# Retention and two feed-forward layers: where the decay is applied and which quarters of the array the states use

## The chip, the cores and the metric

The kernel runs on one core of one Trainium2 chip. The metric is the device time of one execution in microseconds. A page of the profile and a trace of one execution stand beside the times. Engines: PE is TensorE's matmul row, PEld its weight loads, DVE is VectorE, ACT is ScalarE, POOL is GpSimd, SP is SyncE, which here only issues DMAs.

## The reference

Four sequences of 768 tokens, 8 heads of 64, float32. Per head a state is carried through the tokens; then two feed-forward layers of 512 to 2048 to 512 follow on the 3072 tokens.

```python
for t in range(S):
    state = gamma[None, :, None, None] * state + np.einsum('bhd,bhe->bhde', k[:, :, t], v[:, :, t])
    y[:, :, t] = scale * np.einsum('bhd,bhde->bhe', q[:, :, t], state)
...
h = x @ w_in;  g = np.maximum(0.01 * h, h);            x = g @ w_out
h = x @ w_in;  g = h * (1.0 / (1.0 + np.exp(-1.702 * h)));  x = g @ w_out
```

## The kernel before, in words

**Retention.** The tokens go in 24 steps of 128 (4 sequences of 6 chunks, `s` is the step, `c` its chunk within the sequence). The 8 heads are 4 pairs `n` of two halves `e`; a pair's two heads of 64 fill the 128 partitions. A step has four groups of matmuls in float32, each of which the trace shows as 16 instructions, two for each of 8 products:

- `a_scores` (L252): keys by queries, 64 rows by 128 columns of the array, into the PSUM tiles `s0` and `s1`. VectorE multiplies each by the decay mask (`sm`, L256).
- `kv` (L283): decayed keys by values, accumulated through a sequence; VectorE multiplies it by a decay to the next state `st` (L298). GpSimd decays the keys beforehand (L267).
- `o` by `sm` (L289): values by masked scores, 128 rows by 64 columns of the array.
- `o` by state (L295): state by queries, 64 by 64 of the array, added into the same `o`. It is there where `c > 0`, in 20 of the 24 steps. Head half `e = 0` lies on rows and columns 0 to 63, `e = 1` on 64 to 127, so two of the array's four quarters are used. The queries were multiplied by their decay before (`qs`, L263, VectorE, two steps ahead).

`a_store` copies `o` out of PSUM with ScalarE. The tile `o` has two buffers. The first four steps' tokens go straight into the split tile `x0` (a high part by ScalarE, L307, and the rest by VectorE, L308); later steps go to DRAM by pairs (L314, L316). From step 4 on one feed-forward group, `ffn_in(0, m)` (L204, 12 matmuls of 512 columns), follows in each step but 8, 13, 18 and 23.

**Weights.** The feed-forward weights come as 64-bit floats and are converted to a pair of float32r parts, one block of 128 by 512 at a time. `work()` (L183) is one conversion: it issues the load for two conversions later (`load_raw`), then `convert` (ScalarE L139, L140; VectorE L141, L142, L144, L146), then `finish` of the conversion before (ScalarE's high part L125, GpSimd's low part L126), then `round_in` (an integer addition on GpSimd, L152). It is called in retention steps 2 to 4 and then in the steps that follow a feed-forward group, 17 times; and 15 times more after the retention, once for each `ffn_out` group of the first block (L486). There two `ffn_out` groups go with one `ffn_in` group until the queue of 10 blocks between them is worked off, near 212 us.

**Order.** Nothing reorders the program: each engine takes its instructions in the order of the source, and waits come from the tiles' buffers. A step `s` of the loop calls: scores of step `s + 1`, `a_out(s)`, `work()` where it is due, `a_store(s)`, the decays for step `s + 2`, the load for step `s + 4`, and the feed-forward group. The memory of the `a_` pools is taken over by the second weight home when the retention is done.

**Start.** The loads stand in SP's queue in this order: queries and keys of step 0, the mask (512 KB), the rest of step 0, the small decays, step 1, the query decay (256 KB), steps 2 and 3, two raw weight blocks. Matmuls on an idle tile fill the gaps.

Of the kernel before, what the change touches and what calls it, by code (L numbers as in the profile page):

```python
# [9 lines left out]
F32 = mybir.dt.float32  # L10
# [73 lines left out]
def retention_two_ffn(ctx: ExitStack, tc: tile.TileContext, qkv, consts, small, w1i, w1o, w2i, w2o, scratch, out):  # L84
# [42 lines left out]

    def load_raw(kind, m, src):
        t = cv_p.tile([P, 512, 2], U32, tag="raw", name="raw", bufs=3)
        nc.sync.dma_start(out=t, in_=src[m].bitcast(U32).rearrange("p (f two) -> p f two", two=2))  # L130
        raw[kind, m] = t
# [51 lines left out]
    def work():  # L183
# [35 lines left out]
    with ExitStack() as actx:  # L219
# [10 lines left out]
        mask = cst[:, :H].rearrange("p (n e) i -> p n e i", e=2)  # L230
# [4 lines left out]
        ins, sc_t, ks_t, qs_t = {}, {}, {}, {}  # L235
# [8 lines left out]
        def a_scores(s):  # L244
# [3 lines left out]
            ps = [ps_a.tile([P, NP, P], F32, tag=f"s{e}", name=f"s{e}") for e in range(2)]  # L248
            for n in range(NP):
                for e in range(2):  # L250
                    r = slice(D * e, D * e + D)
                    nc.tensor.matmul(out=ps[e][:, n], lhsT=kT[r, n], rhs=qT[r, n], start=True, stop=True,  # L252
                                     skip_group_check=True)
# [17 lines left out]
        def a_out(s):  # L271
            b, c = steps[s]
            t = ins.pop(s)
            sm, ks, qs = sc_t.pop(s), ks_t.pop(s, None), qs_t.pop(s, None)
# [10 lines left out]
            o = ps_a.tile([P, NP, P], F32, tag="o", name="o", bufs=2)  # L285
            for n in range(NP):
                for e in range(2):
                    r = slice(D * e, D * e + D)
                    nc.tensor.matmul(out=o[r, n], lhsT=v[:, n, r], rhs=sm[:, e, n], start=(n == 0),  # L289
                                     stop=(c == 0), skip_group_check=True)  # L290
# [11 lines left out]
        def a_store(s, o):  # L302
            blk, cc = divmod(s, CPB)
            cols = slice(cc * P, cc * P + P)
            if blk == 0:

                nc.scalar.copy(out=x0[:, :, 0, cols], in_=o)  # L307
                nc.vector.tensor_tensor(out=x0[:, :, 1, cols], in0=o, in1=x0[:, :, 0, cols].bitcast(F32),  # L308
                                        op=ALU.subtract)
                return  # L310
            if cc % 2 == 0:
                a_store.x = a_x.tile([P, NP, 2 * P], F32, tag="x", name="x")
            x = a_store.x
            nc.scalar.copy(out=x[:, :, cc % 2 * P : cc % 2 * P + P], in_=o)  # L314
            if cc % 2:
                nc.sync.dma_start(out=xd0[blk][:, :, cc * P - P : cc * P + P], in_=x)  # L316
# [16 lines left out]
        warm = ps_a.tile([P, 512], F32, tag="o", name="warm", bufs=2)  # L333
# [10 lines left out]
        for s in range(len(steps)):  # L344
# [574 lines left out]
```

## Time and profile before

| | |
|---|---|
| time, median of 3 runs | 1128.59 us (1128.12 to 1129.69) |
| span of the profiled execution | 1127.0 us |
| TensorE busy | 1103.3 us (98%) |
| VectorE busy | 696.4 us (62%) |
| ScalarE busy | 491.5 us (44%) |
| GpSimd busy | 269.8 us (24%) |
| mean DMA rate | 177 GB/s |

The span runs from the first to the last instruction of one profiled execution; the runs are timed as a whole. A matmul's end in the trace is modelled and matmuls overlap, so a busy TensorE is one that has instructions in flight. In a row of a timeline `x16` counts merged instructions, and the bracket at its end tells how long the engine was idle before it and what ended that.

### The profile page before, as it was taken

Reading aid. Unit: us, or ns where it says so; the run is one execution under the profiler, and the core shown is the slowest. Engines: PE = TensorE matmul, PEld = TensorE weight load, DVE = VectorE, ACT = ScalarE, POOL = GpSimd, SP = SyncE. Lnnn points to the kernel's source line nnn. Section 1 sums busy time; section 2 is a strip of 40 time slices with the busy share of each in tenths; the row PEclk is TensorE's granted clock in tenths of the full one; section 3 lists DMA queues with packets and bytes.
Section 4 is the critical chain, followed back from the end, with each engine's and each line's share of the span. In section 5 each row is a group of like instructions: output and inputs, shape, how many; then the busy total and the mean of one; then the engine's idle time right before and its main releaser. Section 6 shows DMA issues by size and latency. Waiting matters only on the chain.

```text
span 1127.0 us, 16412 instructions
## 1 busy us (share of the span) xinstructions
PE 1103.3 (98%) x6188; PEld 940.3 (83%) x6189; DVE 696.4 (62%) x1034; ACT 491.5 (44%) x823; POOL 269.8 (24%) x269
## 2 busy tenths in 40 slices
PE   8999989999999999999999999999999899999997
PEld 6888867788888888888888899999998688888886
DVE  5977769635555556455441557575654696686784
ACT  2544455444444444445442435343432444545543
POOL 2655446523324233232321111111100000000000
PEclk9999989999999999999999999999999999999999
DMA  9898543225454445354359633436289725326322
GB/s 366 313 339 292 181 148 113 75 89 164 130 179 154 153 157 175 122 172 137 121 174 426 232 113 114 168 113 243 99 282 359 261 76 176 123 76 205 106 64 74
DMA packets 88095, 199.03 MB, mean 177 GB/s; under 512 B 7888, under 2 KB 51920, under 8 KB 82640
## 3 DMA queue, kind: packets, MB, share of 16 engines
q1 hardware_dynamic: 69584, 172.81, 43.9%
q10 hardware_dynamic: 18432, 25.17, 6.2%
q8 instruction: 48, 0.79, 0.3%
q14 instruction: 31, 0.25, 0.1%
HBM read 125.60 MB, written 72.35 MB: 176 GB/s over the span
## 4 chain that ended last, share of the span: by engine, by line
PE 91%; DVE 4%; DMA 2%; issue 1%; ACT 1%; POOL 0%; SPq 0%; ACTq 0%; DVEq 0%; POOLq 0%
PE h L204 22%; PE y L486 22%; PE b L576 9%; PE a L576 6%; PE d L759 6%; PE f L759 6%; PE c L576 6%; PE e L759 5%; PE h L759 3%; PE s L252 2%; PE o L289 2%; PE o L295 2%; PE kv L283 1%; DMA home<-wdo 1%; DVE raw L141 1%
## 5 line engine op out<-in xcount | busy, mean ns | idle before, releaser
L486 PE MATMUL y<-g,home 128*128 128x512 f32 x1008 | 246.2, 395 | 6.5 <-ACT home L125 3.8
L204 PE MATMUL h<-xs,home 128*128 128x512 f32 x1008 | 246.5, 394 | 0.0
L486 PEld LDWEIGHTS y<-g,home 128*128 128x128 f32 x1008 | 190.4, 189 | 50.8 <-POOL home L126 5.1
L204 PEld LDWEIGHTS h<-xs,home 128*128 128x128 f32 x1008 | 188.5, 188 | 43.2 <-issue 2.4
L126 DVE TENSOR_TENSOR g<-h,g 128x512 fp32r<-128x512 f32 x96 | 101.4, 1057 | 156.4 <-ACT g L125 156.2
L710 ACT CAST op<-g 128x512 fp32r<-128x512 f32 x168 | 100.9, 621 | 90.1 <-DVE g L737 42.4
L715 DVE TENSOR_TENSOR op<-g,op 128x512 fp32r<-128x512 f32 x168 | 112.1, 686 | 40.4 <-ACT op L710 39.7
L209 ACT ACTIVATE h<-h 128x512 f32<-128x512 f32 x96 | 57.3, 597 | 170.3 <-PE h L204 168.2
L576 PE MATMUL b<-xf,home 128*128 128x384 f32 x576 | 115.4, 334 | 2.0 <-DVE g L606 1.4
L576 PEld LDWEIGHTS b<-xf,home 128*128 128x128 f32 x576 | 101.1, 188 | 2.7 <-DVE g L606 1.7
L404 POOL TENSOR_TENSOR f<-f,raw 128x512 int32<-128x512 int32 x32 | 41.7, 1303 | 247.6 <-DVE f L400 247.6
L125 ACT CAST g<-h 128x512 fp32r<-128x512 f32 x96 | 59.6, 621 | 78.6 <-PE y L486 78.1
L576 PE MATMUL a<-xf,home 128*128 128x384 f32 x384 | 76.9, 334 | 0.0
L576 PE MATMUL c<-xf,home 128*128 128x384 f32 x384 | 76.9, 334 | 0.0
L759 PE MATMUL d<-op,home 128*128 128x512 f32 x288 | 69.0, 398 | 5.7 <-DVE op L715 5.7
L737 DVE TENSOR_TENSOR g<-g 128x512 f32<-128x512 f32 x96 | 72.3, 753 | 1.9 <-DMA g<-gd 1.9
L410 POOL TENSOR_TENSOR f<-f 128x128 f32<-128x128 f32 x128 | 72.0, 581 | 5.0
L759 PEld LDWEIGHTS d<-op,home 128*128 128x128 f32 x288 | 54.8, 191 | 18.0 <-DVE op L715 6.1
L759 PE MATMUL e<-op,home 128*128 128x512 f32 x288 | 69.3, 395 | 0.1
L576 PEld LDWEIGHTS a<-xf,home 128*128 128x128 f32 x384 | 67.5, 188 | 0.1
L576 PEld LDWEIGHTS c<-xf,home 128*128 128x128 f32 x384 | 67.5, 188 | 0.0
L759 PE MATMUL f<-op,home 128*128 128x512 f32 x288 | 66.9, 391 | 0.0
(94 smaller groups left out, 1400.3 us busy)
## 6 DMA issues: line engine op xcount, KB each, us to landing
gd<-g ACTq DMA_DIRECT2D x128, 192.0 KB, 2.0
g<-gd SPq DMA_DIRECT2D x96, 256.0 KB, 4.6
in<-qkv SPq DMA_DIRECT2D x21, 1024.0 KB, 6.9
home<-wdi SPq DMA_DIRECT2D x8, 1792.0 KB, 13.0
home<-wdo SPq DMA_DIRECT2D x8, 1792.0 KB, 9.8
raw<-w1i SPq DMA_DIRECT2D x16, 512.0 KB, 5.6
raw<-w1o SPq DMA_DIRECT2D x16, 512.0 KB, 3.3
raw<-w2i SPq DMA_DIRECT2D x32, 256.0 KB, 3.6
```

What stands on the lines that cost most here:

```text
L125: nc.scalar.copy(out=hi, in_=src)
L126: (eng or nc.vector).tensor_tensor(out=lo, in0=src, in1=hi.bitcast(F32), op=ALU.subtract)
L204: nc.tensor.matmul(out=h, lhsT=w[:, a, k], rhs=xs[k][:, c], start=(i == 0), stop=(i == 3 * NP - 1))
L209: nc.scalar.activation(out=t, in_=h, func=AF.Lrelu)
L404: nc.gpsimd.tensor_tensor(out=self.f.bitcast(I32), in0=self.f.bitcast(I32), in1=self.low.bitcast(I32), op=ALU.add)
L410: nc.gpsimd.tensor_tensor(out=f[:, o], in0=f[:, a], in1=f[:, b], op=ALU.subtract)
L486: nc.tensor.matmul(out=y[j], lhsT=w[:, a, j * P : j * P + P], rhs=g[:, c], start=(m == 0 and i == 0), stop=(m == KF - 1 and i == 2))
L576: nc.tensor.matmul(out=t, lhsT=w[:, k, a], rhs=x[:, b, k], start=(start and m == 0), stop=(m == 5), skip_group_check=True)
L710: nc.scalar.copy(out=t[:, 0], in_=block_of(raw, *item))
L715: nc.vector.tensor_tensor(out=t[:, 1], in0=block_of(raw, *item), in1=t[:, 0].bitcast(F32), op=ALU.subtract)
L737: nc.vector.tensor_tensor(out=a(*s[0]), in0=a(*s[1]), in1=a(*s[2]), op=s[3])
L759: nc.tensor.matmul(out=t[:, j], lhsT=w[:, j, a], rhs=x[:, b], start=(new and q == 0 and m == 0), stop=(q == NQ - 1 and m == 2), skip_group ...
```

## The change

- The query decay is no longer applied to the queries. Both parts of `o` are made without it, and `a_store` multiplies by it on VectorE while it copies `o` out of PSUM, for every step. In the first four steps ScalarE's high part and VectorE's rest are then taken from that copy.
- The mask then holds only a key's own decay, which is a column of the small table; GpSimd makes the mask on chip from it with one `affine_select`, and the mask's load goes. The small table is issued first, on ScalarE's queue.
- In `o`, odd pairs are put on the swapped halves of the partitions, so that the state products of two neighbouring pairs use the four quarters of the array; even and odd pairs go to different PSUM banks. `o` takes two banks and has one buffer. The rows of the first layer's input weights, and the query decay, are loaded with halves swapped for odd pairs, by three DMAs (`swapped`).
- The two score tiles are one, with one `sm` operation of 1024 elements.
- `round_in` runs on VectorE.
- Where a step has a conversion, `a_store` is called inside `work`, after `convert` and before `finish` and `round_in`.

```diff
+    def swapped(d, s):
+        nc.sync.dma_start(out=d[:, 0::2], in_=s[:, 0::2])
+        for e in range(2):
+            nc.sync.dma_start(out=d[D * e : D * e + D, 1::2], in_=s[D * (1 - e) : D * (1 - e) + D, 1::2])
...
-        nc.gpsimd.tensor_tensor(out=a.bitcast(I32), in0=a.bitcast(I32), in1=t[:, :, 0].bitcast(I32), op=ALU.add)
+        nc.vector.tensor_tensor(out=a.bitcast(I32), in0=a.bitcast(I32), in1=t[:, :, 0].bitcast(I32), op=ALU.add)
...
         if n < len(order):
             convert(*order[n])
+        between()
         if 0 < n <= len(order):
             kind, m = order[n - 1]
             finish(kind, m)
...
-            ps = [ps_a.tile([P, NP, P], F32, tag=f"s{e}", name=f"s{e}") for e in range(2)]
+            ps = ps_a.tile([P, 2, NP, P], F32, tag="s", name="s")
...
-            for e in range(2):
-                nc.vector.tensor_tensor(out=sm[:, e], in0=ps[e], in1=mask[:, :, e], op=ALU.mult)
+            nc.vector.tensor_tensor(out=sm, in0=ps, in1=mask, op=ALU.mult)
...
-            if c > 0:
-                qs_t[s] = a_t.tile([P, NP, P], F32, tag="qs", name="qs")
-                nc.vector.tensor_tensor(out=qs_t[s], in0=ins[s][:, 0].rearrange("p (n i) -> p n i", n=NP),
-                                        in1=qdec, op=ALU.mult)
...
-            o = ps_a.tile([P, NP, P], F32, tag="o", name="o", bufs=2)
+            o = ps_a.tile([P, 2, 512], F32, tag="o", name="o")
+            out = lambda n, e: o[D * (e ^ (n & 1)) : D * (e ^ (n & 1)) + D, n % 2, n // 2 * P : n // 2 * P + P]
...
-                        nc.tensor.matmul(out=o[r, n], lhsT=st[c % 2][r, n], rhs=qs[r, n], start=False, stop=True,
+                        nc.tensor.matmul(out=out(n, e), lhsT=st[c % 2][r, n], rhs=q[r, n], start=False, stop=True,
...
+            if cc % 2 == 0:
+                a_store.x = a_x.tile([P, NP, 2 * P], F32, tag="x", name="x")
+            x = a_store.x[:, :, cc % 2 * P : cc % 2 * P + P]
+            nc.vector.tensor_tensor(out=x.rearrange("p (m u) i -> p u m i", u=2),
+                                    in0=o[:, :, : 2 * P].rearrange("p u (m i) -> p u m i", i=P),
+                                    in1=qdec.rearrange("p (m u) i -> p u m i", u=2), op=ALU.mult)
             if blk == 0:
-                nc.scalar.copy(out=x0[:, :, 0, cols], in_=o)
-                nc.vector.tensor_tensor(out=x0[:, :, 1, cols], in0=o, in1=x0[:, :, 0, cols].bitcast(F32),
+                nc.scalar.copy(out=x0[:, :, 0, cols], in_=x)
+                nc.vector.tensor_tensor(out=x0[:, :, 1, cols], in0=x, in1=x0[:, :, 0, cols].bitcast(F32),
                                         op=ALU.subtract)
                 return
-            nc.scalar.copy(out=x[:, :, cc % 2 * P : cc % 2 * P + P], in_=o)
...
+        nc.scalar.dma_start(out=smalls, in_=small)
         nc.sync.dma_start(out=ins[0][:, :2], in_=qkv[0, :, :2])
-        nc.sync.dma_start(out=cst[:, :H], in_=consts[:, :H])
         nc.sync.dma_start(out=ins[0][:, 2:], in_=qkv[0, :, 2:])
-        nc.sync.dma_start(out=smalls, in_=small)
+        nc.gpsimd.affine_select(out=cst[:, :H], in_=kdec[:, 0].unsqueeze(2).to_broadcast([P, H, P]),
+                                pattern=[[0, H], [1, P]], base=0, channel_multiplier=-1,
+                                compare_op=ALU.is_ge, fill=0.0)
         a_load(1)
-        nc.sync.dma_start(out=cst[:, H:], in_=consts[:, H:])
+        swapped(qdec, consts[:, H:])
...
             if s >= W0 - 2 and done[0] < KF + 1 and (s <= W0 or now_in[s - 1]):
-                work()
-            a_store(s, o)
+                work(lambda: a_store(s, o))
+            else:
+                a_store(s, o)
```

## Rows read from the trace of the kernel before

**Rows 1.** The page: the chain that ended last, shares of the span by engine.
```profile
PE 91%; DVE 4%; DMA 2%; issue 1%; ACT 1%; POOL 0%; SPq 0%; ACTq 0%; DVEq 0%; POOLq 0%
```

**Rows 2.** Windows: length, busy us of PE, PEld, DVE, ACT, POOL; clock, DMA.
```profile
0.00:30.00 30.00, 26.77 (x335) 19.18 (x338) 18.03 (x31) 7.86 (x12) 8.59 (x12) 1.00 0.95 369
30.00:58.00 28.00, 28.00 (x335) 22.69 (x330) 26.33 (x41) 14.06 (x23) 19.14 (x15) 1.00 0.86 311
58.00:141.00 83.00, 83.00 (x964) 67.27 (x963) 60.43 (x96) 35.16 (x62) 42.38 (x32) 1.00 0.75 268
141.00:212.00 71.00, 64.52 (x263) 50.62 (x262) 60.64 (x73) 39.68 (x68) 42.73 (x29) 0.95 0.35 118
...
300.00:350.00 50.00, 50.00 (x220) 41.11 (x219) 29.68 (x41) 24.15 (x39) 14.96 (x21) 1.00 0.49 160
```

**Rows 3.** Timeline, retention step 8: start us, us, engine, line, operation.
```profile
54.17 0.41 DVE L298 TENSOR_TENSOR st<-kv,smalls 128x256 f32<-128x256 f32 x1
...
54.35 0.85 PEld L295 LDWEIGHTS o<-qs,st 64*64 64x64 f32 x16 [0.17 <-issue]
...
54.50 1.31 DVE L141 TENSOR_SCALAR raw<-raw 128x512 uint32<-128x512 uint32 x1
...
56.64 0.69 DVE L146 SCALAR_TENSOR_TENSOR a<-a,raw 128x512 uint32<-128x512 uint32 x1
...
56.98 1.04 PE L289 MATMUL o<-sm,in 128*64 128x128 f32 x16
```

**Rows 4.** Windows of line L295 alone at its start: busy PE, PEld; clock, DMA.
```profile
17.32:17.34 0.02, 0.01 (x2) 0.01 (x2) 1.00 0.50 205
17.35:17.48 0.13, 0.13 (x2) 0.13 (x4) 1.00 1.08 441
```

**Rows 5.** Groups by line, 0 to 212 us: count, busy us, mean ns, idle before.
```profile
L152 POOL TENSOR_TENSOR a<-a,raw 128x512 int32<-128x512 int32 x31 | 48.9, 1576 | 43.4 <-DVE a L146 37.3 <-ACT raw L140 6.2
L486 PE MATMUL y<-g,home 128*128 128x512 f32 x168 | 43.9, 414 | 6.5 <-ACT home L125 3.8 <-POOL home L126 2.7
L126 POOL TENSOR_TENSOR home<-a,home 128x512 fp32r<-128x512 f32 x28 | 39.4, 1409 | 39.1 <-ACT home L125 39.0
...
L256 DVE TENSOR_TENSOR sm<-s,cst 128x512 f32<-128x512 f32 x48 | 30.9, 684 | 25.8 <-PE s L252 25.7
```

**Rows 6.** Timeline of the first steps, up to the first feed-forward group.
```profile
20.29 1.28 DVE L256 TENSOR_TENSOR sm<-s,cst 128x512 f32<-128x512 f32 x2
...
26.60 1.28 POOL L126 TENSOR_TENSOR home<-a,home 128x512 fp32r<-128x512 f32 x1
...
30.21 1.40 DVE L263 TENSOR_TENSOR qs<-in,cst 128x512 f32<-128x512 f32 x1
...
30.59 3.05 PE L204 MATMUL h<-xs,home 128*128 128x512 f32 x12
...
31.53 1.27 DVE L256 TENSOR_TENSOR sm<-s,cst 128x512 f32<-128x512 f32 x2
```

**Rows 7.** Timelines of retention steps 13 and 18, and the next step's `o`.
```profile
85.29 0.69 DVE L146 SCALAR_TENSOR_TENSOR a<-a,raw 128x512 uint32<-128x512 uint32 x1
...
85.37 1.04 PE L289 MATMUL o<-sm,in 128*64 128x128 f32 x16
...
113.76 1.04 PE L289 MATMUL o<-sm,in 128*64 128x128 f32 x16
...
114.41 0.69 DVE L146 SCALAR_TENSOR_TENSOR a<-a,raw 128x512 uint32<-128x512 uint32 x1
```

**Rows 8.** Timeline after the retention, two conversions.
```profile
200.14 1.69 POOL L152 TENSOR_TENSOR a<-a,raw 128x512 int32<-128x512 int32 x1 [0.63 <-DVE a L146]
200.59 1.53 DVE L141 TENSOR_SCALAR raw<-raw 128x512 uint32<-128x512 uint32 x1
...
202.04 0.42 DVE L142 TENSOR_SCALAR a<-a 128x512 f32<-128x512 f32 x1
...
209.28 1.69 POOL L152 TENSOR_TENSOR a<-a,raw 128x512 int32<-128x512 int32 x1 [0.63 <-DVE a L146]
```

More of the change, by code (lines that the diff above doesn't have):

```diff
@@ L126, in split @@
         (eng or nc.vector).tensor_tensor(out=lo, in0=src, in1=hi.bitcast(F32), op=ALU.subtract)
+    def swapped(d, s):
+        nc.sync.dma_start(out=d[:, 0::2], in_=s[:, 0::2])
+        for e in range(2):
+            nc.sync.dma_start(out=d[D * e : D * e + D, 1::2], in_=s[D * (1 - e) : D * (1 - e) + D, 1::2])
     def load_raw(kind, m, src):
         t = cv_p.tile([P, 512, 2], U32, tag="raw", name="raw", bufs=3)
-        nc.sync.dma_start(out=t, in_=src[m].bitcast(U32).rearrange("p (f two) -> p f two", two=2))
+        if kind == "i":
+            d, s = (a.rearrange("p (k f) -> p k f", k=NP) for a in
+                    (t.rearrange("p f two -> p (f two)"), src[m].bitcast(U32)))
+            swapped(d, s)
+        else:
+            nc.sync.dma_start(out=t, in_=src[m].bitcast(U32).rearrange("p (f two) -> p f two", two=2))
         raw[kind, m] = t
@@ L181, in retention_two_ffn, with work @@
     done = [0]
-    def work():
+    def work(between=lambda: None):
         n = done[0]
@@ L229, in retention_two_ffn @@
         cst = a_c.tile([P, H + NP, P], F32, name="cst")
-        mask = cst[:, :H].rearrange("p (n e) i -> p n e i", e=2)
+        mask = cst[:, :H].rearrange("p (n e) i -> p e n i", e=2)
         qdec = cst[:, H:]
@@ L234, in retention_two_ffn @@
         steps = [(b, c) for b in range(B) for c in range(NC)]
-        ins, sc_t, ks_t, qs_t = {}, {}, {}, {}
+        ins, sc_t, ks_t = {}, {}, {}
         kv_t = {}
@@ L251, in a_scores @@
                     r = slice(D * e, D * e + D)
-                    nc.tensor.matmul(out=ps[e][:, n], lhsT=kT[r, n], rhs=qT[r, n], start=True, stop=True,
+                    nc.tensor.matmul(out=ps[:, e, n], lhsT=kT[r, n], rhs=qT[r, n], start=True, stop=True,
                                      skip_group_check=True)
             sm = a_t.tile([P, 2, NP, P], F32, tag="sm", name="sm")
-            for e in range(2):
-                nc.vector.tensor_tensor(out=sm[:, e], in0=ps[e], in1=mask[:, :, e], op=ALU.mult)
+            nc.vector.tensor_tensor(out=sm, in0=ps, in1=mask, op=ALU.mult)
             sc_t[s] = sm
@@ L273, in a_out @@
             t = ins.pop(s)
-            sm, ks, qs = sc_t.pop(s), ks_t.pop(s, None), qs_t.pop(s, None)
+            sm, ks = sc_t.pop(s), ks_t.pop(s, None)
+            q = t[:, 0].rearrange("p (n i) -> p n i", n=NP)
             v = t[:, 3].rearrange("p (n f) -> p n f", n=NP)
@@ L288, in a_out @@
                     r = slice(D * e, D * e + D)
-                    nc.tensor.matmul(out=o[r, n], lhsT=v[:, n, r], rhs=sm[:, e, n], start=(n == 0),
+                    nc.tensor.matmul(out=out(n, e), lhsT=v[:, n, r], rhs=sm[:, e, n], start=(n < 2),
                                      stop=(c == 0), skip_group_check=True)
@@ L304, in a_store @@
             cols = slice(cc * P, cc * P + P)
+            if cc % 2 == 0:
[4 more added lines that the diff above has]
+                                    in1=qdec.rearrange("p (m u) i -> p u m i", u=2), op=ALU.mult)
             if blk == 0:
-                nc.scalar.copy(out=x0[:, :, 0, cols], in_=o)
-                nc.vector.tensor_tensor(out=x0[:, :, 1, cols], in0=o, in1=x0[:, :, 0, cols].bitcast(F32),
+                nc.scalar.copy(out=x0[:, :, 0, cols], in_=x)
+                nc.vector.tensor_tensor(out=x0[:, :, 1, cols], in0=x, in1=x0[:, :, 0, cols].bitcast(F32),
                                         op=ALU.subtract)
                 return
-            if cc % 2 == 0:
-                a_store.x = a_x.tile([P, NP, 2 * P], F32, tag="x", name="x")
-            x = a_store.x
-            nc.scalar.copy(out=x[:, :, cc % 2 * P : cc % 2 * P + P], in_=o)
             if cc % 2:
-                nc.sync.dma_start(out=xd0[blk][:, :, cc * P - P : cc * P + P], in_=x)
+                nc.sync.dma_start(out=xd0[blk][:, :, cc * P - P : cc * P + P], in_=a_store.x)
             if s == 2 * CPB:
@@ L332, in retention_two_ffn @@
         nc.vector.memset(idle, 0.0)
-        warm = ps_a.tile([P, 512], F32, tag="o", name="warm", bufs=2)
+        warm = ps.tile([P, 512], F32, tag="h", name="warm")
         def keep_warm(n):
```

1 line of the change is left out of this document (added).

## The prediction

> **What bounds the kernel now.** I read the page's chain of waits first: TensorE is 91% of it, so only what stops or shortens TensorE's row of instructions can move the end [rows 1]. Then the windows by stage, since the change touches only the first 212 us [rows 2]: from 212 us on nothing is edited, and I let that part only slide. From 30 to 141 us TensorE's busy time equals the window, so there the retention, with the first feed-forward block laced in, is TensorE-bound; it lacks 3.2 us of work before 30 us and 6.5 us between 141 and 212. The second number to see is VectorE: 26.33 of 28 us between 30 and 58, against 60.4 of 83 afterwards. It is full beside a full TensorE, and every VectorE edit in that window has no room. Last the timelines of single steps, to see who waits at a step's seam.
>
> **The change, part by part.**
>
> *Queries by state in quarters.* One step's group is 16 instructions over 0.85 us behind a 0.17 us switch [rows 3]. The counted windows show how they run: two start together, and those two alone run for the next 0.13 us [rows 4]. So these are eight rounds of two, 0.85/8 = 0.106 us a round. Neighbouring head pairs now use the other two quarters and another PSUM bank; with four at a time four rounds are left, 0.43 us less. At worst the second pair does not start beside the first and nothing is gained; no pass is added, so I see no loss. I take 0.40, near the full gain, since the two quarters used today start within 0.02 us of each other. 20 of 24 steps have a state.
>
> *Decay in the copy out of PSUM.* Twenty `qs` multiplications go (1.40 us where GpSimd blocks them [rows 6]), 24 multiplications come: PSUM times SBUF, 128x512, the shape of one `sm` operation, 0.68 us [rows 5]. For VectorE this is nearly even in sum but not in place: `qs` could run any time in a step, the new one can run only when `o` is complete, and it stands behind the four conversion operations of the step, because `work` calls the store between `convert` and `finish`. It also becomes the only thing that frees `o`, which has one buffer in place of two. So TensorE's next `o` waits for VectorE. Queued behind it on VectorE are `round_in` and the next `sm`. In the first four steps ScalarE must still copy the high part and VectorE then subtract: an idle VectorE of about 0.7 us (estimate: one 0.6 us copy and the hops).
>
> The Trainium skill bears on this: TensorEngine Tiling (Array Packing), PSUM Bottleneck, says that array tiling does not speed up the emptying of PSUM, and that both ScalarE and VectorE should be used for it. By that rule the second rival below is the likely end; the rows here show the crowding on VectorE that it warns of, but no wait on `o` yet.
>
> *Integer addition on VectorE.* 31 additions of 1.58 us leave GpSimd in the first 212 us [rows 5]; each costs VectorE what its nearest two-input 4-byte operation L146 costs unblocked, 0.69 us [rows 3]. Bounds: 0.42, a one-input operation's time [rows 8], and 1.40, as the blocked `qs` [rows 6].
>
> *Mask on chip, one `sm` operation for two.* A 512 KB load leaves the head of the queue; GpSimd makes the mask while the first loads land and TensorE does the first scores, so I cost it at nothing; were it late, the first `sm` would slip by up to two GpSimd operations, some 2 us. The smaller queue front brings the fourth `sm` forward by 0.5 (bounds 0 and 1.4, 512 KB at the 369 GB/s of that window [rows 2]). One `sm` in place of two saves a start-up, 0.06 us.
>
> *Swapped loads.* 16 weight loads and the decay table become three DMAs each, 34 more issues on SP, in pieces of 1 KB and less. SP has nothing to do but issue; a raw tile is loaded two conversions ahead, some 9 us [rows 8], and the DMA share is 0.86 and then 0.75 [rows 2]. I cost it at nothing. Uncovered, a load that lands 1 us late would delay a conversion by as much, in 16 places; I keep 2 us of that for the range.
>
> **The sum.**
> 1. *First steps, late by 3.0.* From the `sm` at 20.29 to the one two steps later at 31.53 VectorE runs nearly without a break: 11.24 us [rows 6]. Two `qs` go (1.40 each, by the row); two multiplications, two waits for ScalarE and two integer additions come, 2 x (0.68 + 0.70 + 0.69) = 4.14; minus 0.12 for `sm`. 11.24 - 2.80 + 4.14 - 0.12 = 12.5, from 19.8, so the second `sm` stands at 32.3. ScalarE's copy of the fourth step comes ahead of its copy of the first weights, so GpSimd's low part, at 26.60 today, starts only after the addition, at 32.3, and takes 1.3: the first feed-forward group goes from 30.59 to 33.6.
> 2. *Sixteen later steps with a state*, 16 x 0.40 = -6.4. The earlier four are inside term 1.
> 3. *Three new waits, 4.5.* Where a conversion step has no feed-forward group behind it (steps 8, 13 and 18), TensorE comes back to `o` after only scores and `kv`. Step 8: L146 ends at 57.33, the multiplication at 58.01; TensorE would be there at 56.98 - 0.40: 1.4 [rows 3]. Step 13: 85.98 + 0.68 against 85.37 - 0.40: 1.7; step 18, which has no state: 115.10 + 0.68 against 113.76: 2.0 [rows 7]. 0.2 off each because GpSimd is clear of the addition: 4.5. In the other steps a feed-forward group of 12 and the scores lie between, about 4 us, and hide the wait; if VectorE falls behind by that much the cover is gone (second rival).
> 4. *Stage from 141 to 212, -2.7.* TensorE waits 3.8 us once for a landing, which stays, and 2.7 us in all for GpSimd's low parts [rows 5]. The pace there is 9.14 us for two conversions, and L141 at 200.59 ends only after GpSimd's addition has ended [rows 8]: VectorE and GpSimd take turns. The VectorE operations of a conversion, three of 0.42 [rows 8] and two of some 0.69, sum to 2.6 and GpSimd's two to 3.0 [rows 5], and the pace of 4.57 means that 1.0 of that overlaps, half a microsecond a GpSimd operation. Afterwards 3.3 + 1.4 - 0.5 = 4.2, close to what TensorE needs (36 matmuls for two conversions at the steady pace of a later window, 50 us for 220 [rows 2], 4.1 each). So the 2.7 goes; what is late next is TensorE itself. Bounds 0 and -2.7.
>
> The Trainium skill, SBUF — State Buffer, Who interferes with whom, says that a VectorE operation with two SBUF inputs and a GpSimd operation that reads SBUF exclude each other. The stretched L141 agrees. By that rule without any overlap the new pace would be 4.7, no better than now, and term 4 would be nothing: 1129.7, the upper end of the forecast's own range.
>
> +3.0 - 6.4 + 4.5 - 2.7 = -1.6, so a span of 1125.4 after 1127.0. The median of the runs, 1128.59, stands 1.6 above the profiled span; I carry that over: 1127.0.
>
> **Rivals.**
> *VectorE gets free in time (faster, 30%).* If GpSimd with one operation less is out of the way, L141 takes 0.42 and not 1.31 [rows 3, 8]; 0.9 off each of the three waits, and 1.5 off the first delay: -1.6 - 2.7 - 1.5, 1122.8; with the waits gone altogether 1121 and below, to 1118. For it: GpSimd loses half of its work per conversion. Against: the L141 stretch at 54.50 comes from GpSimd's low part, which stays. I set it at 1121.
>
> *The single `o` holds every conversion step (slower, 20%).* From the point where a conversion step's VectorE work (0.41 + 1.22 + 2.0 + 0.68 + 0.69 = 5.0, plus what GpSimd blocks) exceeds TensorE's step of some 5.6 us (28 us for five steps [rows 2]), the multiplication is late by the rest in each step. Between 30 and 58 VectorE has only 1.67 us free [rows 2] and gets 0.63 a step more, five steps: 3.2, of which half finds no room, and the later ten steps lose about 0.2 each. If TensorE then stands idle long enough to fall to half its clock, that costs what it does between 141 and 212, where it waits 3.8 us in one piece and the granted clock is 0.95: 0.05 x 71 = 3.5 us lost [rows 2, 5]. -1.6 + 1.6 + 2 + 3.5 = +5.5: 1134. For it: the full VectorE. Against: in the first 30 us TensorE's gaps, 3.2 us in all, leave the granted clock at 1.00 [rows 2].
>
> *The quarters don't run side by side (12%).* The change then does not do what it says: +6.4, less 0.8 of waits that shrink: 1132.6. For it: the profile shows two quarters at once, never four. Against: nothing in it orders them by pairs.
>
> **How the numbers follow.** The forecast has 38%, its own range 1124 to 1130. About 0.2% (2.3 us) is what a measurement of this kernel can tell from no change. Faster: the first rival's 30% and 8% of the forecast. Same: 29% of the forecast and 2% of the third rival. Slower: 20% and 10% of the rivals and 1% of the forecast. The range reaches to both sides, 1119.5 to 1133.5; it leaves out the far end of the first rival and the second where the clock falls as well.
>
> **What would show it.** Right: the L295 group at about 0.45 us; the first L204 group near 33.6; `o` matmuls waiting for VectorE in three steps by 1 to 2 us; no wait for GpSimd's low part after 170 us. Wrong: L295 still 0.85; no wait at step 8; VectorE-made waits in every step; a granted clock under 1 before 141.

## The result, and the profile after

The changed kernel takes **1135.72 us** (median of 4 runs, 1133.33 to 1136.06) against 1129.14 us of the kernel before on the same chip: ratio 1.0055, 95% interval 1.0040 to 1.0069. That is slower, 2.2 us above the predicted range. The profiled execution spans 1134.3 us.

The chain of waits of the kernel after, shares of the span by engine, answers to [rows 1]. TensorE has gone from 91% to 84%, VectorE from 4% to 9%: something now ends on VectorE.

```profile
PE 84%; DVE 9%; DMA 3%; issue 2%; ACT 1%; POOL 0%; SPq 0%; DVEq 0%; ACTq 0%; POOLq 0%
```

The windows of the kernel after (columns as in [rows 2]):

```profile
0.00:30.00 30.00, 22.98 (x321) 15.88 (x324) 16.44 (x26) 6.10 (x10) 6.51 (x10) 1.00 0.97 316
30.00:58.00 28.00, 25.02 (x270) 19.27 (x268) 26.73 (x34) 12.20 (x21) 11.21 (x9) 0.94 0.83 255
58.00:141.00 83.00, 75.68 (x928) 60.05 (x925) 69.18 (x93) 23.53 (x42) 26.90 (x22) 0.96 0.87 293
141.00:212.00 71.00, 65.23 (x349) 51.60 (x348) 59.75 (x89) 39.34 (x68) 17.79 (x13) 0.98 0.37 127
```

Read PE first. In [rows 2] it was 28.00 of 28 and 83.00 of 83; now 3.0 us and 7.3 us are missing, although the quarters gave it less to do. The granted clock, 1.00 there before, is 0.94 and 0.96: (1 - 0.94) x 28 + (1 - 0.96) x 83 = 5.0 us lost.

Which matmuls wait is in the groups by line of TensorE, 0 to 152 us (count, busy us, mean ns, idle us before and what ended it). L298 is `o` by `sm` (L289 before), L317 the new multiplication out of PSUM:

```profile
L264 PE MATMUL s<-in 64*128 64x128 f32 x384 | 27.9, 285 | 5.1 <-DMA in<-qkv 2.7 <-DVE sm L267 2.2
L298 PE MATMUL o<-sm,in 128*64 128x128 f32 x384 | 26.9, 285 | 10.6 <-DVE x L317 10.6
```

10.6 us of waits for L317. One of them, the counterpart of step 8 in [rows 3], in the timeline of the kernel after (L307 is the state, L152 to L157 the conversion, L126 and L274 GpSimd's low part and key decay):

```profile
57.93 1.22 DVE L267 TENSOR_TENSOR sm<-s,cst 128x1024 f32<-128x1024 f32 x1
...
58.75 1.28 POOL L126 TENSOR_TENSOR home<-a,home 128x512 fp32r<-128x512 f32 x1 [3.40 <-ACT home L125]
...
58.84 0.43 PEld L304 LDWEIGHTS o<-in,st 64*64 64x64 f32 x16 [0.17 <-issue]
...
59.07 0.41 DVE L307 TENSOR_TENSOR st<-kv,smalls 128x256 f32<-128x256 f32 x1
59.40 0.92 DVE L152 TENSOR_SCALAR raw<-raw 128x512 uint32<-128x512 uint32 x1
...
60.00 1.22 POOL L274 TENSOR_TENSOR in<-in,smalls 128x512 f32<-128x512 f32 x1
60.24 1.26 DVE L153 TENSOR_SCALAR a<-a 128x512 f32<-128x512 f32 x1
...
61.99 0.69 DVE L157 SCALAR_TENSOR_TENSOR a<-a,raw 128x512 uint32<-128x512 uint32 x1
...
62.60 0.69 DVE L317 TENSOR_TENSOR x<-o,cst 128x512 f32<-128x512 f32 x1
...
63.34 1.09 PE L298 MATMUL o<-sm,in 128*64 128x128 f32 x16 [2.13 <-DVE x L317]
```

TensorE finished the old `o` at about 59.5; VectorE does the whole conversion first and empties `o` at 62.60 to 63.29. The quarters themselves work: the state group (L304) takes 0.43 us, where [rows 3] had 0.85. The other long waits, from the same timeline of TensorE, are these (a fifth, at 29.43, is of 1.01 us):

```profile
38.43 0.87 PE L298 MATMUL o<-sm,in 128*64 128x128 f32 x10 [2.78 <-DVE x L317]
...
92.85 1.32 PE L298 MATMUL o<-sm,in 128*64 128x128 f32 x16 [2.36 <-DVE x L317]
...
124.13 1.22 PE L298 MATMUL o<-sm,in 128*64 128x128 f32 x10 [2.34 <-DVE x L317]
```

Windows of the kernel after, ahead of and behind these waits, show what came with three of them, at 38.43, 92.85 and 124.13: the granted clock is 0.50, the lower level of 1.2 GHz. Behind the wait of 2.13 us at 63.34 it stayed at 1.00.

```profile
35.40:38.90 3.50, 0.72 (x14) 0.53 (x12) 3.43 (x6) 1.36 (x3) 0.91 (x1) 1.00 0.96 281
39.00:42.30 3.30, 3.30 (x29) 2.43 (x26) 3.30 (x3) 0.62 (x1) 2.46 (x2) 0.50 0.73 238
93.60:97.00 3.40, 3.40 (x28) 2.40 (x23) 1.61 (x3) 0.00 (x0) 0.70 (x1) 0.50 0.90 278
124.30:127.70 3.40, 3.40 (x34) 2.64 (x33) 2.42 (x4) 0.00 (x0) 1.04 (x1) 0.50 1.02 416
```

The first steps (answering to [rows 6]), SP's issues and TensorE in the timeline after. A swapped weight block takes three DMAs; the issues of the first two blocks hold SP from 8.06 to 12.66 us, and the input of step 4 is issued behind them, at 13.17 (at 10.56 in the kernel before). Its scores wait for it at 23.23. The first feed-forward group still starts at 31.06.

```profile
8.06 0.58 SPq L130 DMA_DIRECT2D raw<-w1i  x1
9.46 1.26 SPq L132 DMA_DIRECT2D raw<-w1i  x2
...
13.17 0.33 SPq L254 DMA_DIRECT2D in<-qkv  x1
...
23.23 1.16 PE L264 MATMUL s<-in 64*128 64x128 f32 x16 [2.70 <-DMA in<-qkv]
...
30.63 1.30 POOL L126 TENSOR_TENSOR home<-a,home 128x512 fp32r<-128x512 f32 x1 [6.32 <-ACT home L125]
...
31.06 0.73 PE L216 MATMUL h<-xs,home 128*128 128x512 f32 x2
...
32.41 1.21 DVE L267 TENSOR_TENSOR sm<-s,cst 128x1024 f32<-128x1024 f32 x1
```

After the retention, the groups of TensorE by line from 141 to 212 us, beside L486 in [rows 5]: the waits for GpSimd's low part are 0.7 us instead of 2.7, the wait for the landing 5.1 instead of 3.8.

```profile
L501 PE MATMUL y<-g,home 128*128 128x512 f32 x149 | 37.6, 405 | 5.8 <-ACT home L125 5.1 <-POOL home L126 0.7
```

And two conversions there on VectorE (timeline, answering to [rows 8]). The pace is 4.40 us a conversion instead of 4.57; the stretched operation is now the second (L153) instead of the first, beside GpSimd's low part; the addition (L163) takes 0.69.

```profile
200.79 0.42 DVE L152 TENSOR_SCALAR raw<-raw 128x512 uint32<-128x512 uint32 x1
201.13 1.53 DVE L153 TENSOR_SCALAR a<-a 128x512 f32<-128x512 f32 x1
...
203.98 0.69 DVE L163 CUSTOM_DVE_ANT_0 a<-raw,a 128x1024 uint16<-128x1024 uint16 x1
...
205.19 0.43 DVE L152 TENSOR_SCALAR raw<-raw 128x512 uint32<-128x512 uint32 x1
```

**The account between the two traces.** The last feed-forward group of the retention starts at 140.4 before and at 150.3 after: 9.9 us late. The first was 0.5 late; between them come quarters, 16 x 0.42 = -6.7, waits on `o` without the first one, +9.6, and the clock, +5.0: 8.4 in sum, so 1.5 us are left over. Of these, 0.4 is a wait for `sm` at 120.02 and 0.2 one for the low part within the first group; the two clocks are rounded to 0.01, which can be 0.6 us; the rest is not assigned. Then the landing, +1.3, GpSimd's low parts, -2.0, and the clock from 141 to 212, lost 0.05 x 71 = 3.5 before and 0.02 x 71 = 1.4 after, -2.1: 9.9 - 2.8 = 7.1. Counted back from the end, ScalarE's copy that starts at 272.5 us in the kernel before starts 7.16 us later in the kernel after, and from there to 870 us this lag moves by 0.2 us (in the other runs by up to 2.0). I call it the lag at 272 us. It is used below because it leaves out what comes behind the edited part, falls of the clock among it, by which the lag still moves up to 3.9 us in one execution (number 7).

### The profile page after: what moved, and what is told of

It reads as the page before. It is cut to its first block, busy times and chain, and to the rows that moved or that the text cites. A ratio compares the mean times of both kernels' runs of the same rounds, so it can differ in the third digit from the quotient of the medians.

```text
span 1134.3 us, 16403 instructions
## 1 busy us (share of the span) xinstructions
PE 1097.9 (97%) x6188; PEld 933.8 (82%) x6189; DVE 710.2 (63%) x1046; ACT 480.3 (42%) x803; POOL 219.5 (19%) x238
## 3 DMA queue, kind: packets, MB, share of 16 engines
q10 hardware_dynamic: 18576, 25.21, 6.1%
## 4 chain that ended last, share of the span: by engine, by line
PE 84%; DVE 9%; DMA 3%; issue 2%; ACT 1%; POOL 0%; SPq 0%; DVEq 0%; ACTq 0%; POOLq 0%
PE y L501 21%; PE h L216 21%; PE b L591 8%; PE d L774 6%; PE f L774 6%; PE a L591 5%; PE c L591 5%; PE e L774 5%; PE h L774 3%; DVE a L153 2%; DMA gd<-g 1%; DVE raw L152 1%; PE o L298 1%; DVE a L157 1%; DVE sm L267 1%
## 5 line engine op out<-in xcount | busy, mean ns | idle before, releaser
L126 DVE TENSOR_TENSOR g<-h,g 128x512 fp32r<-128x512 f32 x96 | 100.6, 1048 | 148.1 <-ACT g L125 147.9
```

The costliest lines, as they stand in the source:

```text
L126: (eng or nc.vector).tensor_tensor(out=lo, in0=src, in1=hi.bitcast(F32), op=ALU.subtract)
```

## The experiments

The theory (A) is that the multiplication that empties `o` stands behind the conversion on VectorE, and that the next step's first matmul waits for it because `o` has one buffer. The rivals are that VectorE simply has too much to do in a conversion step, the swapped transfers, the addition, and the clock. Each time stands with its ratio to the kernel before on the same chip. The intervals reach 1 to 3 us to either side, so differences of 1 us between rows are not told apart; the lag is that of the one profiled execution.

| kernel | us | ratio, 95% interval | lag at 272 us |
|---|---|---|---|
| the change | 1135.72 | 1.0055 [1.0040, 1.0069] | +7.2 |
| 1. multiplication first | 1127.93 | 0.9991 [0.9980, 1.0001] | -0.2 |
| 2. `o` in halves | 1134.87 | 1.0062 [1.0044, 1.0079] | +6.6 |
| 3. addition on GpSimd | 1134.89 | 1.0044 [1.0025, 1.0063] | +5.5 |
| 4. swap in the layout | 1135.34 | 1.0064 [1.0047, 1.0081] | +5.4 |
| 5. addition on GpSimd, swap in the layout | 1129.90 | 1.0007 [0.9998, 1.0016] | -0.7 |
| 6. single transfers, `o` as before | 1130.01 | 1.0008 [0.9999, 1.0017] | -0.1 |
| 7. fillers in the waits | 1137.45 | 1.0071 [1.0045, 1.0097] | +5.8 |
| 8. key decay ahead | 1136.20 | 1.0060 [1.0040, 1.0080] | +5.8 |
| 11. multiplication first, swap in the layout | 1123.90 | 0.9955 [0.9941, 0.9968] | -4.8 |
| 12. the same, raw weight later | 1123.98 | 0.9955 [0.9941, 0.9968] | -7.4 |
| 13. multiplication first, swap in the layout, addition on GpSimd | 1123.50 | 0.9949 [0.9934, 0.9963] | -5.1 |
| 14. number 13, single transfers, `o` as before | 1128.75 | 1.0004 [0.9995, 1.0013] | -1.7 |
| 9. the quarters alone, on the kernel before | 1124.71 | 0.9960 [0.9949, 0.9971] | -4.1 |
| 10. the same, addition on VectorE | 1124.10 | 0.9958 [0.9945, 0.9971] | -4.5 |

**1. The multiplication ahead of the conversion.** One call moved:

```diff
+        between()
         if n < len(order):
             convert(*order[n])
-        between()
```

> The changed kernel with one move: the store's multiplication stands ahead of the conversion on VectorE, not behind it. Theory A (TensorE loses its time waiting for the one buffer of o, which is emptied only behind the four conversion operations; the trace of the changed kernel has 11.4 us of such waits after steps 3, 4, 8, 13 and 18, and three falls of the clock behind them, 5 us): the waits go, the falls go, and about 1122 us come out (1119 to 1127). Rival B (VectorE has too much to do, wherever the multiplication stands): the multiplication now makes VectorE wait for the end of o in every conversion step, about 1 us each, and the time is 1136 or more.

Measured 1127.93, 7.8 us less than the change. By line, TensorE from 0 to 145 us and VectorE from 58 to 141 in this kernel:

```profile
L298 PE MATMUL o<-sm,in 128*64 128x128 f32 x384 | 26.2, 280 | 0.0
```

```profile
L152 DVE TENSOR_SCALAR raw<-raw 128x512 uint32<-128x512 uint32 x11 | 7.4, 675 | 0.0
L153 DVE TENSOR_SCALAR a<-a 128x512 f32<-128x512 f32 x11 | 6.3, 571 | 0.0
```

No wait on `o` is left. And the conversion itself got shorter: in the changed kernel the same two groups were

```profile
L267 DVE TENSOR_TENSOR sm<-s,cst 128x1024 f32<-128x1024 f32 x14 | 17.1, 1220 | 10.3 <-PE s L264 10.3
L152 DVE TENSOR_SCALAR raw<-raw 128x512 uint32<-128x512 uint32 x11 | 13.2, 1196 | 0.0
L153 DVE TENSOR_SCALAR a<-a 128x512 f32<-128x512 f32 x11 | 12.2, 1111 | 0.0
```

1.06 us less a conversion: the multiplication, which reads PSUM, now lies beside GpSimd's work, and the two SBUF operations come later. The L267 row (10.3 us of VectorE waiting for scores) speaks against a VectorE that is too full in this stretch. The time is just above A's range: waits for `sm` (4.8 us) and 3.7 us more ahead of the scores of step 4 now show, and A's "the falls go" held only from 30 to 141 us (clock 1.00): in the first 30 us the clock is 0.89 (1.00 in the change), which is up to 3.3 us.

**2. `o` in halves of its two banks**, used in turn by the steps:

```diff
-            o = ps_a.tile([P, 2, 512], F32, tag="o", name="o")
+            if s == 0:
+                a_out.o = ps_a.tile([P, 2, 2, 2 * P], F32, tag="o", name="o")
+            o = a_out.o[:, :, s % 2]
```

> The changed kernel with o in two buffers again: each step uses 256 of a bank's 512 columns, so two steps' o share the same two banks. VectorE's order is untouched. Theory A: the 11.4 us of waits on o go, and with them the falls of the clock: about 1121 us (1118 to 1126). Rival B: VectorE is as late as before, so TensorE waits for sm instead of for o: 1132 or more.

Measured 1134.87. The waits stayed, and what ended them too (L300 and L319 are L298 and L317 here):

```profile
L300 PE MATMUL o<-sm,in 128*64 128x128 f32 x368 | 27.7, 299 | 9.5 <-DVE x L319 9.5
```

In this program the first matmul into one half still waits for the multiplication out of the other half of the same banks, so the edit did not take the wait away: inconclusive. Number 6 asks again.

**3. The addition back on GpSimd** (`nc.vector` to `nc.gpsimd` in `round_in`).

> The changed kernel with the integer addition back on GpSimd. Theory A: the addition is behind the multiplication, so it is not in the way of o; what changes there is that the key decay no longer runs on GpSimd right inside the conversion, so the waits on o shrink by some 0.8 us each (3 to 4 us), while the 2.7 us of waits for GpSimd's low parts come back between 150 and 212: 1133 to 1137. Rival B: VectorE loses 0.68 us in each of 17 conversions of the retention and is no longer too full: 1128 or less.

Measured 1134.89. The waits on `o` shrink from 10.6 to 7.0 us, and four waits of about 0.6 us for GpSimd's low part, gone in the change, are back behind 180 us. The time is not told apart from the change's.

**4. The swap made in the layout of the inputs**, so that each weight block and the query decay are one transfer again:

```diff
-        swapped(qdec, consts[:, H:])
+        nc.sync.dma_start(out=qdec, in_=consts[:, H:])
...
+    def halves(a):
+        a = a.reshape(*a.shape[:-1], NP, -1).copy()
+        a[..., 1::2, :] = np.concatenate([a[..., D:, 1::2, :], a[..., :D, 1::2, :]], -3)
+        return a
```

> The changed kernel with the swap of halves in the layout of the inputs, so that weights and query decay come in one DMA each, in whole rows. Theory A: SP's queue gets to the load of step 4 some 2.5 us earlier and TensorE's wait at 20.3 us shrinks from 2.9 to 0.6; the wait on o after step 4 takes back part of it: 1133 to 1135. Rival C (the 1 KB pieces and the 34 more issues are what the change costs): 1130 or less.

Measured 1135.34, not told apart from the change's time. The scores' wait for inputs fell from 2.7 to 1.4 us and the waits on `o` stayed (L259, L293, L312 are L264, L298, L317 here): the gain at the start does not reach the end.

```profile
L259 PE MATMUL s<-in 64*128 64x128 f32 x384 | 28.8, 291 | 3.3 <-DVE sm L262 1.9 <-DMA in<-qkv 1.4
L293 PE MATMUL o<-sm,in 128*64 128x128 f32 x368 | 26.3, 288 | 11.1 <-DVE x L312 11.1
```

**5. Numbers 3 and 4 together.** What is then left as the difference from the quarters alone (number 9) is mainly that VectorE empties `o` behind the conversion, with `qs` gone, the mask made on chip and one `sm` operation.

> The changed kernel with the addition back on GpSimd and the swap of halves in the layout of the inputs: against the run of the quarters alone (1124.7 us) there is left, as the difference, that VectorE's multiplication by the query decay empties o, behind the conversion, where ScalarE's copy did (with qs gone from VectorE), and the mask made on the chip. Theory A (who empties o, and behind what, is the largest loss): the runs of the addition alone and of the layout alone took 1.7 and 1.75 us from the end of the input stage of the changed kernel (7.2 us behind the kernel before), so 7.2 - 3.4 = 3.8 us behind: 1133, range 1131 to 1135, with o waits of 1 to 2 us in conversion steps. Rival (the quarters' gain shows as soon as addition and transfers are as before): 1123 to 1127.

Measured 1129.90: better than A's 1131 to 1135, worse than the rival's 1123 to 1127. TensorE by line, 0 to 145 us, and the windows of 30 to 141 us:

```profile
L293 PE MATMUL o<-sm,in 128*64 128x128 f32 x384 | 25.5, 275 | 6.3 <-DVE x L312 6.3
```

```profile
30.00:58.00 28.00, 25.55 (x308) 20.05 (x308) 24.84 (x35) 12.26 (x20) 18.69 (x16) 1.00 0.76 271
58.00:141.00 83.00, 79.94 (x983) 63.49 (x980) 61.59 (x88) 28.18 (x50) 37.76 (x32) 1.00 0.76 280
```

Alone the two edits took 0.8 and 0.4 us off the time, within the noise, and 1.7 and 1.8 off the lag; together they took 5.8 and 7.9. They do not add. With both, the waits on `o` are 1.0 to 1.8 us each, and the clock stays at 1.00. To number 9 there are still 1129.9 - 1124.7 = 5.2 us. Number 13, which differs from this kernel in the place of the multiplication alone, takes 1123.50: that place is worth 6.4 us here.

**6. `o` as before: one bank, two buffers, two quarters**, on number 4, with the order of the change and the addition on VectorE. Nothing is swapped any more; the transfers stay single.

```diff
-            o = ps_a.tile([P, 2, 512], F32, tag="o", name="o")
-            out = lambda n, e: o[D * (e ^ (n & 1)) : D * (e ^ (n & 1)) + D, n % 2, n // 2 * P : n // 2 * P + P]
+            o = ps_a.tile([P, NP, P], F32, tag="o", name="o", bufs=2)
+            out = lambda n, e: o[D * e : D * e + D, n]
```

> The kernel of the layout swap alone (1135.3 us; 11.1 us of o waits) with o as it was before the change: one bank, two buffers, two quarters of the array. The multiplication stays on VectorE behind the conversion, the addition stays there too. Theory A (the waits need both: the multiplication behind the conversion, and one buffer of o, so that the next step's first matmul waits for it): no o wait above 0.5 us although the order is as in the change; the quarters' 20 x 0.42 = 8.4 us come back on TensorE: 1135.3 - 11.1 + 8.4 = 1132.6, less what of the clock's falls goes: 1128 to 1133. Rival (VectorE's conversion steps are too long by themselves, whatever o's buffers): o waits stay above 5 us in all, 1138 to 1143.

Measured 1130.01, 5.3 us less than number 4, although the state group (L299 here) costs its old time again:

```profile
L293 PE MATMUL o<-sm,in 128*64 128x128 f32 x384 | 25.4, 274 | 0.0
L299 PE MATMUL o<-in,st 64*64 64x128 f32 x320 | 21.8, 275 | 0.0
```

So the waits need both, the multiplication behind the conversion and the single buffer; take away either and they are gone. Four quarters with two buffers in banks of their own were not tried.

**7. Fillers.** Ten matmuls on idle data, results unused, ahead of `o` in steps 5, 9, 14 and 19.

```diff
+            if s in (5, 9, 14, 19):
+                filler = ps.tile([P, 512], F32, tag="h", name="filler")
+                for _ in range(10):
+                    nc.tensor.matmul(out=filler, lhsT=idle[:, :P], rhs=idle, start=True, stop=True, ...)
```

> The changed kernel with ten matmuls on idle data (results unused) ahead of o's in steps 5, 9, 14 and 19, where TensorE waits 2.3 to 2.9 us for L317. Theory A (the wait itself costs 11 us in all, and the falls of the granted clock behind it a further 5 us): the granted clock stays 1.0 from 30 to 141 us, the waits are filled rather than gone, 1129.5 to 1132. Rival C (the falls follow from something else, or cost nothing, since the steps behind them wait for VectorE anyway): 1135 to 1138.

Measured 1137.45; A's 1129.5 to 1132 missed. Windows, 30 to 141 us:

```profile
30.00:58.00 28.00, 27.28 (x313) 20.67 (x310) 27.04 (x35) 13.65 (x22) 11.24 (x9) 1.00 0.90 265
58.00:141.00 83.00, 80.19 (x951) 61.19 (x952) 69.09 (x95) 23.05 (x41) 26.84 (x22) 1.00 0.90 293
```

The clock held at 1.00, and from `o` of step 5 to `o` of step 23 it took 107.8 us (39.09 to 146.84) instead of 110.3 (38.43 to 148.70): of the 5.0 us that the falls cost by the clock, 2.5 came back. Most of the rest went into waits that the change does not have, 0.97 us for the multiplication at 76.35 and 0.79 us for an input at 74.22. Then the clock was lower elsewhere (0.94 in the first 30 us, 0.95 between 141 and 212; 1.00 and 0.98 in the change). The lag at 272 us is 1.4 us better than the change's; the longer time comes from behind it, where the lag grows from 5.8 to 9.7 us by 1000 us.

**8. The key decay ahead of the low part** on GpSimd (`a_decay(s + 2)` called ahead of `a_out(s)`).

> The changed kernel with the key decay (L274) of step s+2 issued on GpSimd ahead of the conversion's part on it instead of behind. Theory A (with the addition gone from GpSimd, the decay lies inside the conversion and stretches L152 and L153, which stand ahead of the multiplication L317): L153 falls from 1.11 to about 0.7 us in steps with a conversion, o's waits shorten by 0.3 to 0.9 us each; but L126 itself starts up to 0.9 us later. 1131 to 1135. Rival (the decay's place is without weight): 1135 to 1137.

Measured 1136.20, the rival's time. VectorE by line, 58 to 141 us:

```profile
L152 DVE TENSOR_SCALAR raw<-raw 128x512 uint32<-128x512 uint32 x11 | 9.8, 888 | 0.0
...
L163 DVE CUSTOM_DVE_ANT_0 a<-raw,a 128x1024 uint16<-128x1024 uint16 x12 | 9.5, 788 | 0.0
L153 DVE TENSOR_SCALAR a<-a 128x512 f32<-128x512 f32 x11 | 8.7, 794 | 0.0
```

L153 shortened (1111 to 794 ns), as did L152 (1196 to 888); others lengthened (L163 681 to 788). TensorE's waits on `o` are 10.3 us against 10.6. Where GpSimd's operations lie decides which VectorE operations are stretched; it is no cure for the order. This run also bears on the clock (windows, 30 to 141 us):

```profile
30.00:58.00 28.00, 25.30 (x298) 19.63 (x294) 26.03 (x35) 12.75 (x21) 11.58 (x9) 1.00 0.84 259
58.00:141.00 83.00, 75.14 (x948) 59.71 (x945) 68.12 (x96) 24.32 (x44) 27.19 (x22) 1.00 0.90 295
```

The clock stayed at 1.00 with waits on `o` of 2.39 us (63.90) and 2.69 us (94.72), though it was 0.89 in the first 30 us. From `o` of step 5 to `o` of step 23 it took 107.0 us, 3.3 less than in the change, although the waits on `o` in between sum to 7.8 us against 6.8. So the length of a wait alone did not decide whether the clock fell.

**9. The quarters alone, on the kernel before**: `o` in two banks with one buffer, emptied by ScalarE as before; `qs`, GpSimd's addition, mask and single transfers as before.

> The kernel before with the quarters alone: o in two banks held once, emptied by ScalarE's copy as before, qs still made on VectorE, addition on GpSimd, single transfers, loaded mask. Theory A (the quarters save 0.42 us in each of 20 state steps; what costs in the change is that VectorE's multiplication, which empties o, stands behind the conversion): ScalarE empties o early, so no long wait of o's first matmuls; L295's PEld group 0.43 us; 1129.1 - 8.4 = 1120.7, range 1118 to 1124. Rival (any single o waits for its own emptying, whoever does it): waits of 1 to 2 us in most steps of 4 to 21 eat the gain: 1127 to 1135.

Measured 1124.71, just outside A's range. Timeline of VectorE and TensorE in this kernel:

```profile
28.87 0.68 DVE L311 TENSOR_TENSOR xs<-o,xs 128x512 fp32r<-128x512 f32 x1
...
29.61 1.76 PE L290 MATMUL o<-sm,in 128*64 128x128 f32 x14 [1.59 <-DVE xs L311]
```

This is the one long `o` wait, and the same mechanism: in the first four steps VectorE too reads `o` (the low part), behind a conversion. Later steps, emptied by ScalarE alone, have none.

**10. Number 9 with the addition on VectorE.**

> The quarters alone on the kernel before (1124.7 us), with the addition on VectorE. Theory A (the four waits of 0.8 to 1.0 us on GpSimd's homes behind 170 us go away; VectorE has qs, two halves of sm and the addition, but o is emptied by ScalarE, so no o wait appears): 1120.5 to 1123.5. Rival (VectorE is then the bound of the conversion steps and sm is late): 1124.5 to 1128.

Measured 1124.10, no difference that can be told from number 9. The four waits for the low part behind 170 us went, but ahead of them, at 147 us, the lag is -0.8 us against -3.8 in number 9: what comes before lost about as much as the low parts gave.

**11. Numbers 1 and 4 together.**

> The changed kernel with both mends together: the multiplication ahead of the conversion on VectorE (as in the first experiment, 1127.9) and the swap of halves made in the layout of the inputs instead of by three transfers each. Theory A: no o wait above 1 us, the wait of the scores of step 4 for its input falls from 3.8 to 1 to 2.5 us: 1124 to 1127. Rival (the gain at step 4 is taken back, as when the layout was changed alone): 1127 to 1129.

Measured 1123.90, at the lower end of A's range. With the order right, the single transfers are worth 4.0 us (4.6 by the lag), where alone they were worth 0.4 (1.8).

**12. Number 11, with the second raw weight issued behind the input of step 4.**

> The kernel with the multiplication first and the layout swap (1123.9 us), with the transfer of the second raw weight issued behind the input of step 4 instead of ahead of it. Theory A (the scores of step 4 wait for their input because the DMA engines are busy 0.9 of the first 30 us and the raw weight is ahead of it): the wait of 2.14 us at 19.8 us falls to 0.5 to 1, 1122 to 1123.5. Rival (the conversion of the second weight is then late, or the wait moves to the steps behind): 1123.5 to 1126.

Measured 1123.98. The wait for that input is 0.4 instead of 2.0 us, but a wait of 2.7 us for `sm` follows at 25.8; the median does not move. The lag does, from -4.8 to -7.4, but the profiled execution is the fastest of the five (1122.22), so this shows no gain.

**13. Number 11 with the addition on GpSimd.**

> The kernel with the multiplication ahead of the conversion and the layout swap (1123.9 us), with the addition back on GpSimd. Theory A (the addition on VectorE costs where VectorE's queue stands ahead of what TensorE waits for, as in the changed kernel, 1.7 us; with the multiplication first, nothing waits behind it, and GpSimd has the homes to write): the waits on GpSimd's homes come back (four of 0.8 us): 1125 to 1128. Rival (the addition costs VectorE 1 us per conversion step in any order): 1121 to 1123.

Measured 1123.50, level with number 11, so neither theory's price for the addition is there. It is faster than the kernel before by 0.5% and than the change by 1.1%; numbers 9 to 12 are not told apart from it. TensorE by line, 141 to 212 us, shows what comes back with GpSimd's addition, waits for the low part of 2.8 us as in [rows 5] (2.7):

```profile
L496 PE MATMUL y<-g,home 128*128 128x512 f32 x168 | 43.8, 413 | 7.7 <-ACT home L125 4.9 <-POOL home L126 2.8
```

**14. Number 13 with `o` as before** (the edit of number 6).

> The kernel with multiplication first, layout swap and addition on GpSimd (1123.5 us), with o in two quarters, one bank and two buffers. Theory A (no o wait is left there, so the quarters are worth nearly the full 20 x 0.42 = 8.4 us of TensorE time; a part goes into the waits for DMA and sm that a slower TensorE does not have): 1129 to 1132. Rival (the quarters' gain is mostly taken back by VectorE and DMA, as the quarters alone, 4.5 us, suggested): 1126 to 1128.5.

Measured 1128.75, between the two ranges: with nothing waiting on `o`, the quarters (and their two banks) are worth 5.2 us of the 8.4, and 3.4 by the lag. The rest is not accounted for one by one. Number 13 has longer waits for an input (1.9 us against 0.6), for the landing (4.9 against 4.0) and for a low part (0.6 at 30.73, against none), and more of the lower clock (0.94 against 1.00 in the first 30 us, 0.95 against 0.98 from 141 to 212).

## Why the prediction was wrong

The step that failed is the third term, "Three new waits, 4.5". The mechanism is the one it named (`o` waits for the multiplication behind the conversion; numbers 1 and 6), the size was not: 10.6 us of waits, at five places instead of three, and falls of the clock that the forecast left out.

| term | predicted | measured |
|---|---|---|
| 1, first steps | +3.0 | +0.5 |
| 2, sixteen steps with quarters | -6.4 | -6.7 |
| 3, waits on `o` | +4.5 | +6.8 in the three steps, +3.8 in two others, +5.0 by the clock |
| 4, 141 to 212 us | -2.7 | -2.0 by GpSimd, -2.1 by the clock, +1.3 by the landing |

- *Size of a wait.* For step 8 the working gave 3.66 us from the start of the state group to the end of the multiplication, and 2.23 us until TensorE is back. In the row of the step above it is 58.84 to 63.29, 4.45 us, and 63.34 - 2.13 - 58.84 = 2.37. The prediction took "0.2 off each because GpSimd is clear of the addition". The move of the addition did the opposite: with it back on GpSimd, the waits were 7.0 us instead of 10.6 (number 3). With the addition gone, the key decay (60.00) follows directly on the low part, and the conversion's first pair took 0.92 + 1.26 instead of 1.31 + 0.42. That is 0.45 of the 0.79 us. The other 0.4 is VectorE's state operation, which starts 0.23 us behind the state group instead of 0.18 ahead of it.
- *Where there are waits.* "In the other steps a feed-forward group of 12 and the scores lie between, about 4 us, and hide the wait". At step 5 they lay between and did not: L317 ended 2.78 us after TensorE was back, in the window where VectorE is busy 26.73 of 28 us. Here the second rival's condition, VectorE behind by more than a group, held.
- *The clock.* The forecast had none of its falls in the retention; the second rival had 3.5 us. Three came, 5.0 us by the windows, of which 2.5 to 3.3 came back where there were none (numbers 7 and 8). No run shows what decides whether the clock falls behind a wait.
- *Transfers "at nothing".* "SP has nothing to do but issue" was wrong by position: 4.6 us of issues for two blocks stood ahead of the input of step 4 (2.70 us wait at 23.23, 1.42 with single transfers). In the change itself mending this gave only 0.4 us, within the noise, with the order right 4.0 (number 11).
- *What held.* The quarters (0.43 us a group; the third rival is out), the mask on chip (the first `sm` starts at 6.28 us instead of 6.99), the low parts' waits gone behind 170 us.
- *The first term.* VectorE's part came as forecast: the `sm` that was put at 32.3 starts at 32.41. But the low part that the first group needs did not start "only after the addition, at 32.3": `finish` is called ahead of `round_in`, and the low part is that of the block before. It started at 30.63, and the group at 31.06 instead of 33.6.
- *The rivals.* The first, VectorE free in time (1121), did not come: GpSimd's smaller load did not free VectorE. The second gave 1134, close to the time, with a cause half right: not a lack of VectorE time over the whole retention (10.3 us of it wait for scores from 58 to 141), but its order against a single buffer.

The Trainium skill, TensorEngine Tiling (Array Packing), PSUM Bottleneck, which the prediction cited, bids one use both ScalarE and VectorE for emptying PSUM. The runs agree in part: emptied by ScalarE, number 9, 1124.7; by VectorE behind a conversion, number 5, 1129.9. But emptied by VectorE ahead of it, number 13, 1123.5: between numbers 5 and 13 the place in the queue decided, not the engine. The stretched L141, which the prediction holds up for the rule on two SBUF inputs, has one input (`raw<-raw` in [rows 8]): it shows that a one-input operation is stretched too, and does not test that rule.

What remains open is the part of the 1.5 us not assigned above, what makes the clock fall behind one wait and not behind another, and why edits 3 and 4 give so much more together than alone: their trace shows shorter waits without a fall of the clock, but no run separates the two.

## What to carry to other kernels

An operation that frees a PSUM buffer belongs ahead of bulk work in its engine's queue, above all when the change takes the second buffer away; either remedy alone removed the waits here. Before a blocking operation is moved off an engine, look at what follows next in that queue: it may collide with the same neighbour. Savings need not add: the same edit gave 0.4 us in one kernel and 4.0 in another, and two that gave 0.8 and 0.4 alone gave 5.8 together. So undo parts in pairs, too.

## What the runs showed of the hardware

- Sixteen 64 by 64 float32 instructions (8 products), in two quarters 0.85 us, take 0.43 us when two neighbouring pairs use all four quarters and two banks.
- A one-input VectorE operation in SBUF, 0.41 us alone, took 1.26 us beside a two-input GpSimd operation of 1.22 us (L153 at 60.24). The multiplication out of PSUM, 0.69 us, is not stretched there: in the kernel of number 1 it runs so beside the key decay, at 60.77 against 60.58 to 61.63.
- Three transfers held SP's queue for 1.9 to 2.7 us per weight block in the change (at 17.84 us 0.56 for the first and 1.25 for the other two); one transfer of the same block took 0.33 to 0.42 us in the kernel before (25.21 and 17.87).
- In the change the granted clock fell to 0.50 behind waits of 2.34, 2.36 and 2.78 us on `o`, but not behind one of 2.13 us or the wait of 2.70 us for an input at 23.23. In number 8 it stayed at 1.00 behind waits of 2.39 and 2.69 us on `o`; in number 5, with waits up to 1.8 us, it stayed at 1.00 from 30 to 141 us.
